# The third of seven gated products done by halves in the later chunks of a hashed-attention and relu-squared kernel

## The chip, the cores and the metric

The kernel runs on one core of a Trainium2 chip. The metric is the device time of one execution in microseconds (us); lower is better. The core has five engines with a queue of instructions each: TensorE (PE, with its weight loads as PEld), VectorE (DVE), ScalarE (ACT), GpSimd (POOL) and SyncE (SP). Each engine takes its own queue strictly in order. SP, ACT and POOL also issue DMA transfers.

## The reference

The input is attention with hash buckets, followed by a gated layer. Queries and keys get a bucket of six sign bits, scores outside the bucket are masked, and the result `x` (3072 tokens by 512) goes through two matrix products with a squared relu between them:

```python
q_bits = (np.einsum('bhsd,dk->bhsk', q, proj) > 0).astype(np.int64)
...
mask = q_bucket[:, :, :, None] == k_bucket[:, :, None, :]
scores = np.where(mask, scale * np.matmul(q, k.transpose(0, 1, 3, 2)), -1000000000.0)
...
attn = exp(scores - max) / sum
x = np.matmul(attn, v)            # (4, 8, 768, 64) -> (3072, 512)
h = x @ w_in                      # 512 x 2048
r = np.maximum(h, 0.0)
out = (r * r) @ w_out             # 2048 x 512
```

All of it is in fp32. The kernel also looks at how large queries and keys are; where they are too large for its fast way, a flag (`slow`) sends it to a general path behind it. With these inputs the flag stays zero.

## The kernel before

The program has an attention stage (to about 318 us) and then three chunks of 1024 tokens. Each chunk has a **gated stage**, `h = x @ w_in` with the squared relu, and an **output stage**, `project`, the product with `w_out`.

**Products by halves.** A matrix product is cut into halves in all three sizes and done with seven products instead of eight (Winograd's form of Strassen's method). The function `product` writes them as `add(...)` number 0, 1, 4, 3, 5, 6, 2 in order of time, between copies on ScalarE (`one`, `two`, `five`, `three`) and sums on VectorE. A chunk's gated stage has 8 units `r`; a unit is a block of 128 hidden columns from each half of the hidden layer. In chunk 0 a unit is one `product` (`hidden`). In chunks 1 and 2 units come in pairs, `r = n` and `r = 4 + n` for n = 0 to 3 (`hidden_pair`, L1047): five of the seven products are done as they are, with factors from `w_unit`, and two of them (number 1 and number 2) are cut by halves once more (`inner_steps`, L996), for both units of the pair at once, with 7 matmuls 256 columns wide instead of 4 that are 512 wide. The inner steps stand between the outer products, so that copies on ScalarE are done by the time their accumulator is used again. Each inner product needs sums of weight blocks, which `factor_units(n)` (L957) makes once, in chunk 0's output stage: two loads on GpSimd's queue (L961), four sums on VectorE (L587 to L590, `sums_a`), four writes on GpSimd's queue to `w_in_49` in DRAM (L970). `load_inner` fetches them on SP's queue, one pair ahead. `sums_inner` (L986) makes the matching sums of `x`, four VectorE operations 256 wide per product.

**Output stage.** It is cut twice by halves too: seven outer products k = 0 to 6, here called output products, each of seven inner products of 16 matmul records (8 matmuls, each counted twice by the profile). Weights come as tiles `leaf`, seven in a ring, loaded on ScalarE's queue. Within an output product, in VectorE's program order, stand: in chunk 0 and for k = 1 to 4 the factor sums of `factor_units(k - 1)`; then the `hook`, which stands behind the first two inner products and holds `minus(y21, y21, t2)` (L1258), needed by the seventh and last inner product of the same k, and `inner_sums(k + 1)`, needed by the next output product; then sums of the accumulators (L1132). After k = 0 and k = 2 come two long differences and the inner sums of k + 2.

**What sets the order.** The whole program stands in `tc.manual_schedule()`: each engine runs its instructions in the order of the source. Tiles with a name come from pools with a fixed number of buffers (`bufs`); a tile of the same name waits until the earlier one in its buffer has been read. So PSUM tiles `acc0`, `acc1`, `acc2` have two buffers each, and `spare` one of two banks. A DMA that overwrites a tile waits until DMAs that read the tile have landed, and it holds up what is behind it on its queue.

**Guard.** `load_peak` fetches queries and keys in 32 pieces on GpSimd's queue and `peak` reduces them to their largest magnitude on VectorE (L877), two pieces per unit in chunks 1 and 2. `guard` multiplies the two largest and sets the flag.

The functions below are those of the kernel before that the change touches.

Of the kernel before, what the change touches and what calls it, by code (L numbers as in the profile page):

```python
# [8 lines left out]
FP32 = mybir.dt.float32  # L9
# [6 lines left out]
ALU = mybir.AluOpType  # L16
# [18 lines left out]
def kernel(  # L35
# [49 lines left out]
    w_in_49 = p_d.tile([NQ, P, 2, 7, P], FP32, name="w_in_49")  # L85
# [571 lines left out]
    with tc.manual_schedule():  # L657
# [168 lines left out]

        def product(n, w, at, bt, c11, c12, c21, c22, hook=None):
# [13 lines left out]
            def keep(of, name):  # L841
                t = p_r.tile([P, 512], FP32, name=name)[:, 0:w]
                nc.scalar.copy(out=t, in_=acc[of])  # L843
                return t
# [45 lines left out]
        def guard():  # L890
# [3 lines left out]
            for w in range(2):  # L894
# [8 lines left out]
                out=slow, in0=most[:, 0:1], scalar1=most[:, 1:2], scalar2=PLAIN / (scale * D),  # L903
# [52 lines left out]

        def factor_units(n):  # L957
# [9 lines left out]
            for lo, hi, t in (  # L967
                (0, 2, src[0]), (2, 3, src[1][:, :, 1:2]), (3, 5, sums[0]), (5, 7, sums[1])
            ):
                nc.gpsimd.dma_start(out=w_in_49[n, :, :, lo:hi], in_=t)  # L970

        def load_inner(i, n):

            if n < NQ:
                w_inner[i, n] = []
                for j, name in enumerate((("sum0", "sum3"), ("sum2", "sum1"))[n % 2]):
                    t = p_y.tile([P, 4, QN], FP32, name=name).rearrange("p a (b c) -> p (a b) c", c=P)
                    nc.sync.dma_start(out=t[:, 0:7], in_=w_in_49[n, :, j])
                    w_inner[i, n].append(t)

        def quarters_x(i, j):

            b = xs[i][0][:, 2:4, 0:HN] if j == 0 else xs[i][0][:, 0:2, HN:NCH]
            return b[:, 0, 0:QN], b[:, 0, QN:HN], b[:, 1, 0:QN], b[:, 1, QN:HN]

        def sums_inner(i):  # L986

            t_inner[i] = [p_y.tile([P, NQ, QN], FP32, name=f"t{m}", bufs=2) for m in range(2)]
# [7 lines left out]
        def inner_steps(i, n, j):  # L996
# [5 lines left out]
            if i not in snaps:  # L1002
                o = [p_y.tile([P, HN], FP32, name="o", bufs=NOUT) for _ in range(2)]
                snaps[i] = [o[m // 2][:, m % 2 * QN:(m % 2 + 1) * QN] for m in range(4)]
            one, two, three, five = snaps[i]

            def mul(out, a, b, start, stop):
                nc.tensor.matmul(  # L1008
                    out=out, lhsT=w[:, a], rhs=b, start=start, stop=stop, skip_group_check=True
                )  # L1010
# [10 lines left out]
            def step_1():  # L1021
                hs["a2"] = spare("acc3")[:, 0, 0:QN]
# [24 lines left out]
        def hidden_pair(i, n, half):  # L1047

            r = half * NQ + n
            w, bt = w_unit.pop(i * NR + 2 * n + half), factors_x(i)  # L1050
            acc = {m: ps_m.tile([P, 512], FP32, name=f"acc{m}") for m in (0, 2)}

            def add(to, a, b, first, last):
                for f in range(NFT // 2):
                    nc.tensor.matmul(  # L1055
                        out=acc[to], lhsT=w[:, PLACE[a], f], rhs=bt[b](f),
# [4 lines left out]
            def keep(of, name):  # L1061
                t = p_r.tile([P, 512], FP32, name=name)
                nc.scalar.copy(out=t, in_=acc[of])
                return t

            if half == 0:
                load_inner(i, n + 1)
                now[0], now[1] = (inner_steps(i, n, j) for j in range(2))
# [539 lines left out]
```

## Time and profile before

| | |
|---|---|
| three runs | 866.06, 866.54, 868.85 us; median 866.54 |
| profiled execution | 866.6 us; span of its instructions 864.4 us; mean granted TensorE clock 0.997 |
| chunk 0: gated stage, output stage | about 317.8 to 414.0, 414.0 to 499.5 us of the span |
| chunk 1: gated stage, output stage | 499.5 to 592.4, 592.4 to 677 us |
| chunk 2: gated stage, output stage | 677 to 770, 770 to 864 us |
| output products of chunk 0 start at | k=2 439.1, k=3 451.2, k=6 487.5 us |

Times in the profile count from the start of the span. A line of a timeline gives the start, the duration, the engine, the line of the source, the operation with its tiles (output, then inputs), the shape, how many such instructions are merged, and in brackets how long the engine sat idle before and what ended it. A line of the table by windows gives, after the window, the busy time of each engine with its count, then the granted clock, the share of DMA time and the GB/s. "To landing" is the time from a DMA's issue until its data has arrived. L836 and L1055 are the `add` of `product` and of `hidden_pair`, L1008 the inner products, L593 all differences made by `minus`, L1132 all `add_to`.

### The profile page before, as it was taken

The page shows a single profiled execution, that of the slowest core. Times are in us where ns is not written, and L with a number is a line of the kernel's source. Part 1 is how long each engine was busy: PE and PEld are TensorE (multiplying, and loading weights), DVE is VectorE, ACT ScalarE, POOL GpSimd, SP SyncE. Part 2 cuts the span into 40 slices and gives each one's busy share as a digit, 9 for nine tenths or more (in the row PEclk, how much of TensorE's full clock was granted, in tenths as well). Part 3 has the DMA queues.
Part 4 walks back from the last instruction along what each step waited for, and adds up shares of the span by engine and source line. Part 5 has one row for each costly group of instructions (what it writes and reads, how often), then busy time and mean ns, then how long its engine had stood idle before and what let it go on. Part 6 is the DMA issues. An engine that isn't in the chain of part 4 may idle for free.

```text
span 864.4 us, 16743 instructions
## 1 busy us (share of the span) xinstructions
PE 851.6 (99%) x6548; PEld 519.3 (60%) x6548; DVE 749.3 (87%) x1005; ACT 362.3 (42%) x648; POOL 169.4 (20%) x284
## 2 busy tenths in 40 slices
PE   8999999999999999999999999999999999999996
PEld 3544444444444444444788855557888655568885
DVE  5899999999999998988879978888799688888875
ACT  5787777888777752222111133332111233321110
POOL 1321111123221102642132211112001111100003
PEclk9999999999999999999999999999999999999998
DMA  9677898879997518999788854537757645355565
GB/s 206 128 144 153 175 188 197 209 159 252 251 218 210 192 48 281 317 320 291 279 280 261 178 167 157 176 118 261 249 157 191 161 156 175 119 161 159 147 185 99
DMA packets 226629, 168.03 MB, mean 194 GB/s; under 512 B 167112, under 2 KB 184848, under 8 KB 226544
## 3 DMA queue, kind: packets, MB, share of 16 engines
q1 hardware_dynamic: 187744, 87.19, 40.5%
q0 software_dynamic: 16416, 41.95, 15.8%
q10 hardware_dynamic: 22384, 37.76, 14.3%
q8 instruction: 53, 0.87, 0.4%
q14 instruction: 32, 0.26, 0.1%
HBM read 124.52 MB, written 41.68 MB: 192 GB/s over the span
## 4 chain that ended last, share of the span: by engine, by line
PE 95%; DMA 2%; DVE 1%; issue 0%; POOL 0%; ACT 0%; POOLq 0%; DVEq 0%; ACTq 0%
PE acc L836 39%; PE st L430 17%; PE acc L1055 16%; PE xo L485 14%; PE acc L1008 6%; PE tot L534 2%; PE hash L360 1%; DMA leaf<-w_out 1%; DMA bits<-signed 1%; DVE bits L410 0%; DVE feat L344 0%; DVE total L473 0%; POOL bits L396 0%; DVE total L468 0%; PE xo L360 0%
## 5 line engine op out<-in xcount | busy, mean ns | idle before, releaser
L436 ACT ACTIVATE e<-st 128x768 f32<-128x768 f32 x192 | 155.6, 811 | 59.6 <-PE st L430 56.7
L430 PE MATMUL st<-feat 64*64 64x384 f32 x1536 | 157.5, 483 | 1.0 <-DVE feat L329 1.0
L485 PE MATMUL xo<-e,v_nat 64*64 64x385 f32 (+1 forms) x1520 | 157.2, 483 | 0.0
L836 PE MATMUL acc<-b,leaf 128*128 128x256 f32 x600 | 133.4, 379 | 0.4 <-DMA leaf<-w_out 0.4
L836 PEld LDWEIGHTS acc<-b,leaf 128*128 128x128 f32 x600 | 113.7, 190 | 17.2 <-issue 1.4
L473 DVE TENSOR_TENSOR total<-total,e 128x1536 f32<-128x1536 f32 x64 | 111.8, 1747 | 4.4 <-ACT e L436 2.8
L396 POOL DMA_DIRECT2D bits<-signed x120 | 62.2, 522 | 217.1 <-ACT signed L385 217.1
L485 PEld LDWEIGHTS xo<-e,v_nat 64*64 64x64 f32 (+1 forms) x1520 | 56.5, 133 | 67.2 <-issue 59.0
L1055 PE MATMUL acc<-t_x,w_unit 128*128 128x512 f32 x192 | 90.2, 592 | 0.0
L430 PEld LDWEIGHTS st<-feat 64*64 64x64 f32 x1536 | 56.0, 133 | 39.1 <-issue 33.7
L836 PE MATMUL acc<-t,leaf 128*128 128x256 f32 x336 | 76.2, 380 | 0.0
L836 PEld LDWEIGHTS acc<-t,leaf 128*128 128x128 f32 x336 | 63.7, 190 | 9.1 <-DVE t L593 0.5
L920 DVE SCALAR_TENSOR_TENSOR b<-h 128x512 f32<-128x512 f32 x96 | 65.7, 691 | 3.1
L430 PE MATMUL st<-bits 64*64 64x384 bf16 x768 | 65.2, 325 | 0.9 <-DMA bits<-signed 0.5
L1055 PE MATMUL acc<-x,w_unit 128*128 128x512 f32 x128 | 60.1, 592 | 0.0
L836 PE MATMUL acc<-x,w_unit 128*128 128x512 f32 x128 | 56.5, 593 | 0.0
L1055 PEld LDWEIGHTS acc<-t_x,w_unit 128*128 128x128 f32 x192 | 36.5, 190 | 28.9 <-issue 26.8
L836 PE MATMUL acc<-b_t,leaf 128*128 128x256 f32 x240 | 53.8, 379 | 0.0
L1153 POOL DMA_DIRECT2D out_dram<-h x26 | 16.9, 656 | 174.1 <-DVE h L1146 167.0
L843 ACT COPY two<-acc 128x256 f32<-128x256 f32 (+1 forms) x29 | 12.5, 432 | 87.8 <-PE acc L836 78.4
L836 PEld LDWEIGHTS acc<-b_t,leaf 128*128 128x128 f32 x240 | 45.5, 190 | 6.2
L873 POOL DMA_DIRECT2D raw_qk<-in_q_dram x32 | 17.4, 543 | 162.4 <-DVE peaks L877 162.4
(155 smaller groups left out, 1194.8 us busy)
## 6 DMA issues: line engine op xcount, KB each, us to landing
leaf<-w_out ACTq DMA_DIRECT2D x142, 256.0 KB, 3.1
w_unit<-w_in SPq DMA_DIRECT2D x16, 640.0 KB, 3.9
raw<-in_moe_w_in_dram SPq DMA_DIRECT2D x8, 1024.0 KB, 6.9
raw<-in_moe_w_out_dram SPq DMA_DIRECT2D x8, 1024.0 KB, 7.2
w_unit<-w_in SPq DMA_DIRECT2D x8, 896.0 KB, 9.3
w_out<-sums POOLq DMA_DIRECT2D x16, 448.0 KB, 7.9
sum<-w_in SPq DMA_DIRECT2D x16, 448.0 KB, 5.0
v_nat<-in_v_dram SPq DMA_DIRECT2D x16, 384.0 KB, 5.1
```

The lines of the kernel that those rows point to most:

```text
L396: nc.gpsimd.dma_start(out=t[h * D:h * D + NBITS + 1, w, c * HS:(c + 1) * HS], in_=signed[at:at + NBITS + 1, h],)
L430: nc.tensor.matmul(out=st[k * HK:(k + 1) * HK, h, 0:HS], lhsT=src[1][rows, key], rhs=src[0][rows, cut], start=first, stop=not first, skip_ ...
L436: nc.scalar.activation(out=key_of(pr, kt)[:, :, i, 0:HS], in_=st[:, :, 0:HS], func=ACTF.Exp, scale=scale)
L473: nc.vector.tensor_tensor(out=totals[pr], in0=totals[pr], in1=e, op=ALU.add)
L485: return nc.tensor.matmul(out=outs[pr][h * D:(h + 1) * D, c, 0:HS + 1], lhsT=nat[pr, "v_nat"][rows, h, kt * D:(kt + 1) * D], rhs=key_of(pr ...
L534: done = nc.tensor.matmul(out=spares[pr][g * 32:(g + 1) * 32, c2, 0:QS], lhsT=ones[rows], rhs=totals[pr][rows, h, c, c2 * QS:(c2 + 1) * QS ...
L836: nc.tensor.matmul(out=acc[to], lhsT=a(i), rhs=b(i), start=first and i == 0, stop=last and i == n - 1, skip_group_check=True,)
L873: nc.gpsimd.dma_start(out=raw_qk[i][:, w], in_=flat[:, i * n:(i + 1) * n])
L920: nc.vector.scalar_tensor_tensor(out=out, in0=h, scalar=0.0, in1=h, op0=ALU.max, op1=ALU.mult)
L1008: nc.tensor.matmul(out=out, lhsT=w[:, a], rhs=b, start=start, stop=stop, skip_group_check=True)
L1055: nc.tensor.matmul(out=acc[to], lhsT=w[:, PLACE[a], f], rhs=bt[b](f), start=first and f == 0, stop=last and f == NFT // 2 - 1, skip_group_ ...
L1153: queue.dma_start(out=out[at, m0 + a * 32:m0 + (a + 1) * 32].rearrange("(c i) j -> i c j", i=32), in_=ot[a * 32:(a + 1) * 32].rearrange("i ...
```

## The change

In chunks 1 and 2 product number 6 of a pair is done by halves too, as a third set of inner steps. `now` holds three sets, A (product 1), B (product 6) and C (product 2), and `hidden_pair` is rewritten: per half four outer products (0, 3, 4, 5), with the steps of A and the first of B in the first half, the rest of B and those of C in the second. Product 3 gets an accumulator of its own (`acc2`), and `two = two + five` on VectorE replaces the summing of 3 and 6 in PSUM. The inner steps use `acc1` and `acc2` in place of two `acc1`, and the two banks of `spare` in turn. The differences `b_t`, `b12` and the first inner sums of the output stage, which followed each unit, move into `hidden_pair`, in the second half ahead of the last gates.

The factors of product 6 have a tile `t2` of their own with one buffer, and a rhythm of their own in chunk 0's output stage: in the hook of k come, in this order, the four sums of third k - 2 (`sum_third`), its three writes on GpSimd's queue (`keep_third`), and the two loads of third k - 1 (`load_third`). Pairs fetch them into two `leaf` buffers, on SP's queue, and for a chunk's first pair on ScalarE's queue in the hook of k = 6. `sums_inner` makes twelve sums instead of eight. `w_unit` is loaded with four blocks instead of five. The copies `two` and `five` have one buffer instead of two.

The guard's reduction moves from VectorE to ScalarE: `peak` squares a piece in place, with a sum along the row, four times per half; the flag's threshold is changed to fit sums of squares.

```diff
-    w_in_49 = p_d.tile([NQ, P, 2, 7, P], FP32, name="w_in_49")
+    w_in_49 = p_d.tile([NQ, P, 3, 7, P], FP32, name="w_in_49")
...
-            m = 7 if n < NR else 5
+            m = 7 if n < NR else 4
...
+        KEPT = dict(one=2, two=1, three=2, five=1)
...
-        def peak(i):
-
-            nc.vector.tensor_reduce(
-                out=peaks[:, :, i], in_=raw_qk.pop(i), axis=AXL.X, op=ALU.max,
-                apply_absolute_value=True,
-            )
+        def peak(i, w):
+
+            t = raw_qk[i][:, w]
+            nc.scalar.activation(
+                out=t, in_=t, func=ACTF.Square, accum_out=peaks[:, w, i:i + 1]
+            )
...
+        def load_third(n):
+
+            t = p_y.tile([P, NQ, QN], FP32, name="t2").rearrange("p a (b c) -> p (a b) c", c=P)
+            thirds[n] = t
+            for j in range(2):
+                nc.gpsimd.dma_start(
+                    out=t[:, 2 * j:2 * j + 2], in_=w_in_7[j * NQ + n, :, PLACE[6]]
+                )
+
+        def sum_third(n):
+
+            t = thirds[n]
+            sums_a(*(t[:, m] for m in range(8)))
+
+        def keep_third(n):
+
+            t = thirds.pop(n)
+            for lo, hi, a in (0, 2, 0), (2, 3, 3), (3, 7, 4):
+                nc.gpsimd.dma_start(out=w_in_49[n, :, 2, lo:hi], in_=t[:, a:a + hi - lo])
...
+        def load_third_inner(i, n, queue):
+
+            if n < NQ:
+                ts = [p_y.tile([P, NQ, P], FP32, name="leaf", bufs=NLEAF) for _ in range(2)]
+                for m, t in enumerate(ts):
+                    hi = min(4 * m + 4, 7)
+                    queue.dma_start(out=t[:, 0:hi - 4 * m], in_=w_in_49[n, :, 2, 4 * m:hi])
+                w_inner[i, n].append(lambda a: ts[a // 4][:, a % 4])
...
-                a0, a1 = (ps_m.tile([P, 512], FP32, name="acc1")[:, 0:QN] for _ in range(2))
+                a0, a1 = (ps_m.tile([P, 512], FP32, name=f"acc{m}")[:, 0:QN] for m in (1, 2))
...
-                hs["a2"] = spare("acc3")[:, 0, 0:QN]
+                hs["a2"] = last
...
+            A, B, C = (now[c] for c in "ABC")
+            add(acc, 0, "11", True, False)
+            one = keep(acc, "one")
+            if half == 0:
+                A[0]()
+            else:
+                B[2]()
+                C[0]()
+                A[4](1, b11[:, r], one)
+                B[4](0, b12[:, r0], now["two"])
+            mark()
+            other = ps_m.tile([P, 512], FP32, name="acc2")
+            add(other, 3, "t1", True, True)
+            five = keep(other, "five")
+            if half == 0:
+                A[1]()
+            else:
+                B[3]()
+                C[1]()
+                minus(b_t[:, r0], b12[:, r0], b11[:, r0])
+                minus(b12[:, r0], b22[:, r0], b12[:, r0])
+            mark()
+            add(acc, 4, "t2", False, False)
+            two = keep(acc, "two")
+            if half == 0:
+                A[2]()
+                B[0]()
+                A[4](0, b11[:, r], one)
+                nc.vector.tensor_tensor(out=two, in0=two, in1=five, op=ALU.add)
+            else:
+                C[2]()
+                nc.vector.tensor_tensor(out=two, in0=two, in1=five, op=ALU.add)
+                B[4](1, b12[:, r], two)
+                minus(b_t[:, r], b12[:, r], b11[:, r])
+                inner_sums(0, slice(n, n + 1))
+                C[4](0, b21[:, r0], now["three"])
+            mark()
+            add(acc, 5, "t3", False, True)
+            three = keep(acc, "three")
+            if half == 0:
+                A[3]()
+                B[1]()
+                gate_sum(b22[:, r], three, five)
+            else:
+                C[3]()
+                gate_sum(b22[:, r], three, five)
+                minus(b12[:, r], b22[:, r], b12[:, r])
+                C[4](1, b21[:, r], three)
+            mark()
...
                     if k + 1 < 7 and k not in (1, 3):
                         inner_sums(k + 1)
+                    if i == 0 and 1 < k <= NQ + 1:
+                        sum_third(k - 2)
+                        keep_third(k - 2)
+                    if i == 0 and 0 < k <= NQ:
+                        load_third(k - 1)
                     if k == 6 and more:
+                        load_third_inner(i + 1, 0, nc.scalar)
                         sums_inner(i + 1)
```

More of the change, by code (lines that the diff above doesn't have):

```diff
@@ L1061, in keep, with mark @@
             def keep(of, name):
-                t = p_r.tile([P, 512], FP32, name=name)
-                nc.scalar.copy(out=t, in_=acc[of])
-                return t
+                t = p_r.tile([P, 512], FP32, name=name, bufs=KEPT[name])
+                nc.scalar.copy(out=t, in_=of)
+                return t
+            marks = iter([(2 * ((i - 1) * NR + 2 * n + half) + m, c) for m in range(2) for c in range(2)])
+            def mark():
+                peak(*next(marks))
             if half == 0:
@@ L1081, in hidden_pair @@
-            steps[2 - half]()
-            if half == 0:
-                put(0, b11[:, r], one)
-            add(2, 6, "22", False, True)
-            gate_sum(b12[:, r], acc[2], two)
-            steps[3 - half]()
-            if half:
-                put(0, b21[:, n], now["three"])
-            add(0, 5, "t3", False, True)
-            three = keep(0, "three")
-            gate_sum(b22[:, r], three, five)
-            if half:
-                steps[3]()
-                put(1, b21[:, r], three)
@@ L1098 @@
+            mark()
[11 more added lines that the diff above has]
+            mark()
+            now["two"], now["three"] = two, three
         OUTER = (0, b11), (5, b12), (3, b_t), (6, b22), (1, b21), (4, b11), (2, b_t)
@@ L1342 @@
                     hidden_pair(i, s // 2, s % 2)
[L1343 removed]
+                if i == 0:
+                    minus(b_t[:, r], b12[:, r], b11[:, r])
                 if i == 0 and r in WHEN:
```

56 lines of the change are left out of this document (25 added, 31 removed).

## The prediction

> **What bounds the kernel now.** I read the busy times first, then the busy times of chosen windows, then the timelines of TensorE, VectorE and GpSimd in the first output stage, then the time to landing of GpSimd's DMAs there. The page:
>
> ```profile
> PE 851.6 (99%) x6548; PEld 519.3 (60%) x6548; DVE 749.3 (87%) x1005; ACT 362.3 (42%) x648; POOL 169.4 (20%) x284
> ```
>
> TensorE has no gap to win back, so only less matmul work can help. Two windows show how much cover VectorE gives (after PE and PEld the columns are DVE, ACT and POOL):
>
> ```profile
> 460.00:470.00 10.00, 10.00 (x48) 8.79 (x48) 9.69 (x20) 1.12 (x3) 4.37 (x7) 1.00 0.88 295
> ...
> 522.90:546.10 23.20, 23.20 (x70) 12.91 (x69) 19.65 (x34) 7.82 (x19) 4.26 (x8) 1.00 0.49 165
> ```
>
> The second is one pair of the gated layer in a later chunk: VectorE has 3.5 us to spare. The first lies in chunk 0's output stage: 0.3 us to spare in 10. The change also works there. GpSimd's timeline, around output product k=2 (439.1 to 451.2):
>
> ```profile
> 444.90 1.41 POOL L970 DMA_DIRECT2D w_in<-h  x2 [0.43 <-DVE h L589]
> 446.03 1.40 POOL L961 DMA_DIRECT2D h<-w_in  x2
> ...
> 452.97 0.70 POOL L970 DMA_DIRECT2D w_in<-h  x1 [0.39 <-DMA h<-w_in]
> 459.96 1.41 POOL L970 DMA_DIRECT2D w_in<-h  x2 [6.29 <-DVE h L589]
> 461.10 1.39 POOL L961 DMA_DIRECT2D h<-w_in  x2
> ```
>
> GpSimd asks for the next factors (L961) as soon as the previous ones are written, here 12.5 us before VectorE sums them. It works strictly in order and blocks on each wait. VectorE at the same time:
>
> ```profile
> 443.51 0.43 DVE L587 TENSOR_TENSOR h<-h 128x256 f32<-128x256 f32 x1 [3.78 <-DMA h<-w_in]
> ...
> 450.65 4.49 DVE L593 TENSOR_TENSOR b_t<-b,b 128x2048 f32<-128x2048 f32 x2
> 455.05 1.22 DVE L593 TENSOR_TENSOR t<-b 128x1024 f32<-128x1024 f32 x1
> ...
> 458.58 0.42 DVE L587 TENSOR_TENSOR h<-h 128x256 f32<-128x256 f32 x1
> ...
> 460.05 1.22 DVE L593 TENSOR_TENSOR b<-b,t 128x1024 f32<-128x1024 f32 x1
> ```
>
> The factor sums (458.58, four) stand ahead of `minus(y21, y21, t2)` (460.05), which feeds the last inner product of k=3. TensorE:
>
> ```profile
> 451.19 3.62 PE L836 MATMUL acc<-b,leaf 128*128 128x256 f32 x16
> 454.64 3.62 PE L836 MATMUL acc<-t,leaf 128*128 128x256 f32 x16
> 458.10 8.80 PE L836 MATMUL acc<-b,leaf 128*128 128x256 f32 x40
> ```
>
> 16 records take 3.45 us; the first 16 of the 40 are two other inner products, so the last one of k=3 starts at 461.55, and y21 is ready at 461.27: 0.28 us of slack. The same reading gives slack of 3.3, 2.8, 3.7 and 2.3 us at k=2, 4, 5, 6. Landing of L970's writes, then of L961's loads:
>
> ```profile
> DMA to landing us min/median/max: 2.7/3.6/5.8
> ```
> ```profile
> DMA to landing us min/median/max: 5.6/6.2/13.0
> ```
>
> **TensorE's work.** The third product of a pair cost 8 records 512 wide; four take 1.72 us (timeline, L1055), so 3.44. Its seven inner products are 14 records 256 wide, 0.215 each: 3.01. Times 8 pairs (two chunks of four): **-3.44 us**. This stands only if TensorE stays the bound.
>
> **The new rhythm in a pair.** Laid out from 0, with 1.72 us an outer and 0.43 an inner product, a pair takes 22.8 us. VectorE loses four peak reductions (0.947 each) and gains two adds of 0.69 and three of 0.42: 19.65 - 3.79 + 2.64 = 18.5 us, so it has more room. Its longest run of work starts at 20.85 and lasts 9.3 us with the starts 0.34 to 0.72 apart that the timeline shows; the next pair's first sum is then done at 7.75 of its time, and TensorE wants that accumulator at 8.17: no wait, 0.4 to spare. ScalarE gains 8 squares and 5 copies of 0.375 a pair. A square 128x384 with a sum is in no row: between the copy 256 wide (0.37) and the reduction 768 wide (0.95); I take 0.5, nearest to the exponential's 0.81 at 768. The narrowest gap between due copies is 1.3 us, so nothing waits. One new tight place: in the second half `two` is copied with only one inner step (0.86) before the accumulator goes on. From the timeline, end to copy 0.21, copy 0.59: 0.06 to spare, without the hand-back. A wait of 0 to 0.13 us, 8 times: 0 to 1.0, I take **+0.3**. The output sums moved ahead of the last gates take away a stall of 0.14 us at the start of the two later output stages (773.41, where 16 records take 3.59 instead of 3.45): **-0.3**. The unit loads shrink from 640 to 512 KB and 448 KB a pair come on top, at a DMA share of 0.49: hidden. These loads go on SP's queue behind the other inner loads, into leaf buffers whose leaves are read by then; for a chunk's first pair they go on ScalarE's queue, where they wait for the first two leaves of k=6 (read by 490.9) ahead of a copy due at 492.83: hidden. GpSimd's peak loads now wait for ScalarE's squares, which come 6 us or more ahead of the next use (3.3 to land): hidden. With one buffer, `two` and `five` are copied again 4.4 us after their last reading at the closest (490.12, 494.56): hidden, and 0.5 us late, under 0.7 of cover, after the delays below.
>
> **Chunk 0's output stage.** Three things are added. On GpSimd, per n, two loads into `t2` and three writes from it, where `t2` has one buffer. On VectorE four sums 128x128 a time, in the hooks of k=2 to 5: between a reduction of one column (0.28) and the sums of 256 (0.42, starts 0.34 to 0.45 apart); starts of 0.2 to 0.3, 0.95 for four. In the hook of k=6 four more sums of 256, 1.6 us. What matters is the order on GpSimd: writes of third n, which wait for VectorE's sums; loads of third n+1, which wait until those writes have landed, the buffer being the same; and only then the next two loads of L961, which the next factor sums wait for. The early request is gone. Step by step:
>
> - k=1, 2: two more issues (0.57 each) and 256 KB go ahead of L961's loads: the sums at 443.51 come 1.7 us later (1.1 by the issues alone, 2.1 with 256 KB at 267 GB/s). y21 is ready at 447.9, due at 449.5: no wait. The inner sums for k=3 end at 451.3, the first third-sums at T = 452.25.
> - k=3: write at T+0.1, landed 3.6 later, then four issues 0.57 apart, the last landed 6.2 after issue: T+11.66 = 463.9. VectorE alone would be there after 1.0 (three sums) + 4.4 + 3.53 = 461.2. Factor sums 1.47, y21 1.2: 466.6 against 461.55. TensorE waits **5.1**.
> - k=4: third-sums end at 467.45, factors land at 479.1 (VectorE would be free at 467.45 + 4.55 + 2.4 = 474.4), y21 at 481.8 against 461.55 + 12.09 + 5.1 = 478.7: **3.1**.
> - k=5: no factors any more; VectorE alone: 3.5 + 0.95 + 4.2 + 2.4 + 1.2, y21 at 493.9, due then: 0.
> - k=6: 3.5 + 0.95 + 8.8 + 1.2: y21 at 508.3, due at 506.0: **2.3**.
> - Start of chunk 1: the second accumulator of k=6 is read after 12 small sums (4.8) and 1.2 us, at 514.1. The new pair takes that buffer for its second outer product, at 510.0 + 2.6: **1.6**. The old pair took the other buffer first.
>
> Together **+12.1 us**. The last two steps follow from VectorE having no slack after 450 (3.78 us of idle were its only reserve). Bounds: with the shortest landings (2.7, 5.6) each of the two rounds is 1.5 us shorter, +9.1; with 5.8 and 6.2 + 1.5 each is 3.7 longer, +19.5, and the median rows are nearest. After chunk 1's output stage, with idle of 3.0, 1.9, 1.0 and 0.8 us and no factors to sum, the 1.6 us meet room: 0.
>
> The Trainium skill (DMA: Bandwidth & Descriptors, section Anatomy of one DMA) gives such a transfer as about 2.0 us plus its bytes at 436 GB/s; an estimate from that page for 256 KB is 2.6 us, where the rows have 3.6 and 6.2. Were it so, the rival of short transfers below would hold; the rows decide against it.
>
> **Sum** on the profiled execution: 866.6 (span 864.4 and 2.2 around; median 866.54, the same) - 3.44 + 0.3 - 0.3 + 12.1 = **875.3 us**.
>
> **Rivals.**
> - VectorE alone: landings short enough that no factor sum waits, but its own additions still shift it, since it is full. Waits then 2.35 at k=3, 0.7 at k=6, 1.6 at the start of chunk 1: 4.65, and 867.9 us. It needs T+9 instead of T+11.66 at k=3 and T+7 at k=4. Against it: no load of L961 landed in under 5.6.
> - Short transfers, not slower: if every transfer of GpSimd lands in 2.7 us, the shortest row of the writes, the factors come in at 440.5, in the idle time before 443.51, and all third-sums but the last two find room; 0.6 is left at k=6 and 1.6 after: 866.6 - 3.4 + 2.2 = 865.4. The point from which it decides is a landing under about 3.5 us. Were even the last two waits covered, the saving alone would stand: 863.2. For it: writes landed in 2.7; against it the loads' 5.6.
> - ScalarE too slow: if a square takes over 1.3 us, `two` is late in each pair; at 2.0 us by 0.7 x 8 = 5.6 on top: 881. For it: no row has this form; against it: 0.81 for twice the columns.
>
> **How the numbers follow.** GpSimd's queue as worked out 0.74; VectorE alone 0.08; short transfers 0.08 (0.03 of it at 863.2); ScalarE 0.07; no effect anywhere 0.03. The time is that of the first. Of its bounds, 872.4 to 882.8, the upper end is unlikely. The range 867.7 to 880.5 takes in VectorE alone and leaves out under 0.2. A difference under 0.3% (2.6 us) is about what a measurement can't tell from no change: faster than 864.0 gets 0.06, within 0.10 (the rest of short transfers, part of VectorE alone), slower 0.84.
>
> **What would show it.** In the changed profile VectorE should wait about 2.7 us and 4.7 us for DMA of L961's tile ahead of the third and fourth factor sums; GpSimd's load of `t2` should wait for a DMA some 3.6 us; TensorE should wait for VectorE's y21 (L593) by about 5, 3, 0 and 2 us at k=3 to 6 and 1.6 us early in chunk 1. Both gated stages of later chunks should take 91.2 us instead of 92.8 each, with no waits but tenths at `two`. The forecast is wrong if the loads of L961 are issued before the third's writes have landed, if y21 comes before 463, or if a pair takes over 23 us.

## The result and the profile after

The changed kernel takes 872.01 us (median of 7 runs, 871.37 to 876.39); the kernel before took 866.65 beside it: a ratio of 1.0068, 95% interval 1.0049 to 1.0087. It is slower by 5.4 us, where 8.7 were forecast. The profiled execution took 875.85 us (span 873.8); five of the seven runs lie near 872, so two more profiles are read beside it below. They are called the second and the third profile here, this one the first.

Span, busy times and the chain that ended last, from the page of the changed kernel:

```profile
span 873.8 us, 17006 instructions
...
PE 852.8 (98%) x6596; PEld 531.8 (61%) x6596; DVE 749.9 (86%) x1037; ACT 408.2 (47%) x816; POOL 180.3 (21%) x304
...
PE 82%; DMA 6%; DVE 5%; issue 3%; POOL 1%; ACT 0%; SPq 0%; ACTq 0%; DVEq 0%; POOLq 0%
```

TensorE has less to multiply, yet its busy time went from 851.6 up to 852.8: some matmuls became slower. And 6% of the chain that ended last are now DMAs. One pair of chunk 1, as the window of the kernel before was shown:

```profile
535.24:558.12 22.88, 22.88 (x76) 13.98 (x75) 18.95 (x35) 13.59 (x40) 4.26 (x8) 1.00 0.52 176
```

22.88 us without a gap, against 23.20. The pairs do what the change says, and the loss must lie elsewhere. TensorE's timeline around k=3 of chunk 0's output stage (start, duration; in brackets the idle time before and what ended it):

```profile
458.35 3.62 PE L838 MATMUL acc<-b,leaf 128*128 128x256 f32 x16
468.12 7.56 PE L838 MATMUL acc<-b,leaf 128*128 128x256 f32 x24 [6.15 <-issue]
475.52 3.62 PE L838 MATMUL acc<-t,leaf 128*128 128x256 f32 x16
478.97 8.80 PE L838 MATMUL acc<-b,leaf 128*128 128x256 f32 x40
```

TensorE stands still for 6.15 us ahead of the last inner product of k=3. The 24 records that follow take 7.56 us where 24 records after a short wait take 5.42. At k=4 (the row of 40) nothing waits. VectorE's timeline tells what the trace only calls "issue":

```profile
465.33 0.42 DVE L587 TENSOR_TENSOR h<-h 128x256 f32<-128x256 f32 x1 [3.98 <-DMA h<-w_in]
...
466.80 1.22 DVE L593 TENSOR_TENSOR b<-b,t 128x1024 f32<-128x1024 f32 x1
```

The second row is y21 of k=3; it ends at 468.02, and TensorE goes on at 468.12, 0.10 us later (0.10 in the second and third profile too). Ahead of it VectorE waited 3.98 us for a factor load. GpSimd, which issues that load:

```profile
452.71 0.54 POOL L994 DMA_DIRECT2D w_in<-t  x1 [3.50 <-DVE t L590]
457.16 1.07 POOL L981 DMA_DIRECT2D t<-w_in  x2 [3.91 <-DMA w_in<-t]
458.22 1.07 POOL L965 DMA_DIRECT2D h<-w_in  x2
464.40 0.72 POOL L974 DMA_DIRECT2D w_in<-h  x1 [5.11 <-DMA h<-w_in]
...
472.09 1.07 POOL L981 DMA_DIRECT2D t<-w_in  x2 [2.27 <-DMA w_in<-t]
473.15 1.06 POOL L965 DMA_DIRECT2D h<-w_in  x2
476.36 0.72 POOL L974 DMA_DIRECT2D w_in<-h  x1 [2.15 <-DMA h<-w_in]
```

This is the chain of the forecast: a third's last write waits 3.50 us for VectorE's sums (L590), the load of the next third waits 3.91 for that write to land, and only then come the factor loads (L965), at 458.22. In the kernel before they were issued at 446.03. In the next round (from 472.09) the same chain runs faster. The landing of L965's loads, first those of 458.22, then those of 473.15:

```profile
DMA to landing us min/median/max: 5.9/6.2/6.5
```
```profile
DMA to landing us min/median/max: 2.9/3.2/3.5
```

At the start of chunk 1, on TensorE:

```profile
508.38 1.88 PE L1096 MATMUL acc<-x,w_unit 128*128 128x512 f32 x4
512.28 1.13 PE L1049 MATMUL acc<-x,sum 128*128 128x256 f32 x4 [2.02 <-DMA sum<-w_in]
513.24 3.44 PE L1096 MATMUL acc<-t_x,w_unit 128*128 128x512 f32 x4
516.48 1.21 PE L1049 MATMUL acc<-t,sum 128*128 128x256 f32 x4
```

The wait of 2.02 us is for the first factor tile of chunk 1, a transfer on SyncE's queue that the forecast does not name. The four records at 513.24 then take 3.44 us instead of 1.88.

To compare profiles that begin chunk 0's output stage 3 us apart, I use a stretch: from that stage's first matmul (414.01 in the kernel before) to the third row of inner products in chunk 1's first pair (506.42). It is 92.41 us before and 104.28 here: +11.87. The pieces shown come to as much: 6.15 + 2.02 of waits, 2.14 (7.56 - 5.42) and 1.56 (3.44 - 1.88) of slow matmuls. That they meet it exactly is chance: the kernel before has a wait of its own in this stretch, 0.4 us for a weight tile (`leaf`), that this profile has not, and smaller slow rows are left out here.

### The profile page after: what moved, and what is told of

Read it like the earlier page. It is cut to its first block, busy times and chain, and to the rows that moved or that the text cites. A ratio compares the mean times of both kernels' runs of the same rounds, so it can differ in the third digit from the quotient of the medians.

```text
span 873.8 us, 17006 instructions
## 1 busy us (share of the span) xinstructions
PE 852.8 (98%) x6596; PEld 531.8 (61%) x6596; DVE 749.9 (86%) x1037; ACT 408.2 (47%) x816; POOL 180.3 (21%) x304
## 4 chain that ended last, share of the span: by engine, by line
PE 82%; DMA 6%; DVE 5%; issue 3%; POOL 1%; ACT 0%; SPq 0%; ACTq 0%; DVEq 0%; POOLq 0%
PE acc L838 27%; PE st L430 17%; PE xo L485 14%; PE acc L1096 13%; PE acc L1049 8%; DMA h<-w_in 3%; PE tot L534 2%; PE hash L360 1%; DMA w_in<-t 1%; DMA sum<-w_in 1%; DMA qk_nat<-in_k_dram 1%; DVE b L593 1%; DMA bits<-signed 1%; DVE t L593 1%; DVE h L1216 0%
## 5 line engine op out<-in xcount | busy, mean ns | idle before, releaser
L838 PE MATMUL acc<-b,leaf 128*128 128x256 f32 x600 | 135.5, 384 | 6.2 <-issue 6.2
L1096 PE MATMUL acc<-t_x,w_unit 128*128 128x512 f32 x192 | 92.4, 604 | 0.0
L838 PE MATMUL acc<-x,w_unit 128*128 128x512 f32 x128 | 56.5, 593 | 0.0
L1096 PEld LDWEIGHTS acc<-t_x,w_unit 128*128 128x128 f32 x192 | 36.1, 191 | 27.3 <-issue 23.5
L845 ACT COPY one<-acc 128x256 f32<-128x256 f32 (+1 forms) x29 | 12.5, 431 | 85.8 <-PE acc L838 61.8
```

The lines of the kernel that those rows point to most:

```text
L838: nc.tensor.matmul(out=acc[to], lhsT=a(i), rhs=b(i), start=first and i == 0, stop=last and i == n - 1, skip_group_check=True,)
L1096: nc.tensor.matmul(out=to, lhsT=w[:, PLACE[a], f], rhs=bt[b](f), start=first and f == 0, stop=last and f == NFT // 2 - 1, skip_group_check ...
```

## Further profiles of the kernels as they are

> The changed kernel once more, unchanged, for a second profile. Its seven timed runs fall into two groups, 871.4 to 872.3 us and 875.9 to 876.4 us, and the profile shown is of the upper group. GpSimd's queue as the cause: the wait of TensorE at k=3 is there again (6.15 us in the first profile), between 4 and 6.2 us; a profile of the lower group differs by how long TensorE ran at a lower clock after its waits, or by the wait at the start of chunk 1. Rival, a wait elsewhere that the first profile happens not to show: another place appears.

Measured: 874.42 us, a single run. The stretch is 103.27 (+10.86).

> The changed kernel as it is, three rounds on the chip of the other runs (the earlier run meant for this was the kernel before). Median 872 to 874; in the profile a wait of 4 to 6 us for k = 3's inner block behind a VectorE wait of 3 to 4 us for the fourth... factor tile, slow matmuls behind it, and a start of chunk 1 that is 8 to 10 us later than in the kernel before, counted from the start of the output stage.

Measured: 872.23 us (870.75 to 874.03, 4 runs) against 867.88, a ratio of 1.0066 (1.0042 to 1.0091); the profiled run took 870.78, its stretch 101.26 (+8.85). TensorE's waits in the two, from the timelines, with the groups that follow:

```profile
467.84 6.92 PE L838 MATMUL acc<-b,leaf 128*128 128x256 f32 x24 [4.88 <-issue]
507.85 3.20 PE L838 MATMUL acc<-b_t,leaf 128*128 128x256 f32 x8 [2.01 <-issue]
510.84 2.38 PE L1096 MATMUL acc<-x,w_unit 128*128 128x512 f32 x4
```
```profile
464.51 7.10 PE L838 MATMUL acc<-b,leaf 128*128 128x256 f32 x24 [4.29 <-issue]
504.24 1.97 PE L838 MATMUL acc<-b_t,leaf 128*128 128x256 f32 x8 [1.54 <-issue]
508.10 1.13 PE L1049 MATMUL acc<-x,sum 128*128 128x256 f32 x4 [0.18 <-DMA sum<-w_in]
510.08 1.98 PE L1096 MATMUL acc<-t_x,w_unit 128*128 128x512 f32 x4 [0.85 <-DVE tmp L1202]
```

So the wait at k=3 is there in each profile (6.15, 4.88, 4.29), with none at k=4; the forecast's waits at k=6 and for VectorE's reading of the last accumulator (L1202) show when k=3 costs less. In the third profile the factor loads of k=3 landed in 4.2 us (median) and VectorE waited 2.05 for them. Over the three profiles the landing at k=3 (6.2, 5.2 and 4.2 us) goes with the time (875.85, 874.42, 870.78); three points are a hint and no proof.

> The changed kernel as it is, on the chip of the other runs, for a median beside theirs. By the two looks so far (a wait at k = 3 of 6.15 and 4.88 us, 2.2 and 1.6 us of slow matmuls behind it) the spread comes from how long the transfers on GpSimd's queue take: the median is 872 to 874, and the wait at k = 3 is 4 to 6 us again with slow matmuls behind it, none at k = 4. A look with a time near 871.5 should have a wait near 4 at k = 3 or none at k = 6.

The file that ran under this label was the kernel before. It took 868.01 us (866.47 to 871.86, 10 runs), with a stretch of 92.48: the stretch of the kernel before repeats within 0.1 us, while its output stage begins 2.3 us later. What its text above expects of the changed kernel is to be read against the run before it.

## The experiments

**The pairs alone.** In chunk 0's output stage no thirds are summed, loaded or written; the pairs read the second product's factors in their place:

```diff
-                    queue.dma_start(out=t[:, 0:hi - 4 * m], in_=w_in_49[n, :, 2, 4 * m:hi])
+                    queue.dma_start(out=t[:, 0:hi - 4 * m], in_=w_in_49[n, :, 1, 4 * m:hi])
...
-                    if i == 0 and 1 < k <= NQ + 1:
-                        sum_third(k - 2)
-                        keep_third(k - 2)
-                    if i == 0 and 0 < k <= NQ:
-                        load_third(k - 1)
```

> Left out: the making of the third factors in chunk 0's output stage (the four sums, the writes and the loads of each third); the pairs read another product's factors in their place, so the output is not the reference's. All cost in chunk 0's output stage and its aftermath: no wait at k=3, none over 0.5 us at the start of chunk 1 (the last accumulator sum is then read at 501.4, due at 502.1), and only the pairs' saving is left: 866.6 - 3.44 + 0.64 (0.08 a pair at the copy of two, as the first profile shows) - 0.3 = 863.5 us. Rival, the pairs' new rhythm is no gain by itself: 866 us or more.

Measured: 863.83 us (863.21 to 865.33, 10 runs) against 867.11, a ratio of 0.9962 (0.9943 to 0.9982). Its stretch is 92.96 (+0.55), and at k=3 one small wait is left:

```profile
461.47 5.42 PE L838 MATMUL acc<-b,leaf 128*128 128x256 f32 x24 [0.22 <-issue]
```

The new rhythm of the pairs is a gain of 3.3 us, and the making of the thirds costs all the rest, some 8.4 us at the medians (872.23 - 863.83), or 7.6 where each is first compared with the kernel before that ran beside it (867.88 and 867.11).

**The factor loads first.** The same work, but the next product's factor loads are issued ahead of the thirds' writes and loads on GpSimd's queue (`load_factors` holds the two loads that stood in `factor_units`):

```diff
+                if i == 0 and k == 1:
+                    load_factors(0)
...
+                    if i == 0 and 0 < k < NQ:
+                        load_factors(k)
                     if i == 0 and 1 < k <= NQ + 1:
                         sum_third(k - 2)
                         keep_third(k - 2)
```

> The two loads for the next factor sums are issued ahead of the third's writes and loads, as early as in the kernel before; nothing else changes. GpSimd's queue as the cause: VectorE no longer waits for these loads ahead of the third and fourth factor sums, the wait at k=3 falls from 6.15 us to about 0.5 (0.95 us of third sums less 0.28 of slack), with 0.7 at k=6 and 2 at the start of chunk 1: 866.7 us. Rival, VectorE's added sums are the cause: the order on GpSimd makes no difference, 872 us.

Measured: 868.08 us (864.74 to 872.45, 10 runs), ratio 1.0002 (0.9976 to 1.0028); the profiled run took 865.18. TensorE's longest waits in it, at k=3, at k=6 and for chunk 1's first factor tile:

```profile
461.58 5.42 PE L838 MATMUL acc<-b,leaf 128*128 128x256 f32 x24 [0.50 <-issue]
498.88 1.97 PE L838 MATMUL acc<-b_t,leaf 128*128 128x256 f32 x8 [0.80 <-issue]
503.15 1.13 PE L1055 MATMUL acc<-x,sum 128*128 128x256 f32 x4 [0.58 <-DMA sum<-w_in]
```

With all transfers and sums kept and only their order changed, the wait at k=3 falls from between 4.3 and 6.2 us to 0.50, and some 4 us come back at the median (872.23 - 868.08; 3.4 by the kernel before beside each). VectorE, which kept the sums, has no wait for a factor load at k=3 or k=4 in this profile. So the order of GpSimd's queue is the cause of the wait at k=3, and of about half of the cost at the median. It does not explain all: 4.2 us above the run without thirds remain (2.0 between the two profiled runs), with a spread of 7.7 us.

**TensorE kept busy.** Four idle products of 512 columns into a spare bank ahead of the last inner product of k=3, to see what the slow matmuls behind the wait cost:

```diff
+                def fill():
+                    void = spare("fill")[:, 0]
+                    for _ in range(4):
+                        nc.tensor.matmul(out=void, lhsT=ident, rhs=b[:, 0], start=True, stop=True)
...
+                    fill if (i, k) == (0, 3) else None,
```

> Four idle matmuls 512 wide (3.44 us, result unused) are put on TensorE ahead of the last inner product of k=3, inside its wait. If the slow matmuls after the wait (24 records in 7.56 us instead of 5.34) come from the idle time, the idle time left is under 3 us, the matmuls run at full rate and 2.2 us go: about 870 us. If the idle time has nothing to do with it, or if the wait is no wait for VectorE: 872 us or, where the fill does not fit, up to 875.

Measured: 873.94 us (871.31 to 876.03, 10 runs), ratio 1.0074 (1.0051 to 1.0097); stretch +9.69. TensorE's timeline:

```profile
461.31 3.60 PE L1352 MATMUL fill<-b,ident 128*128 128x512 f32 x8
465.86 5.42 PE L838 MATMUL acc<-b,leaf 128*128 128x256 f32 x24 [0.95 <-issue]
479.93 5.42 PE L838 MATMUL acc<-b,leaf 128*128 128x256 f32 x24 [1.75 <-issue]
506.42 3.01 PE L838 MATMUL acc<-b_t,leaf 128*128 128x256 f32 x8 [2.03 <-issue]
```

The records behind k=3 run at full rate, as the text above expected where the idle time is the cause, but the 870 us that went with it are a miss: TensorE now waits 1.75 us at k=4 and 2.03 at k=6, and no time is won. In this profile the y21 of k=4 ends at 479.84 and TensorE goes on at 479.93. So VectorE's chain sets the end there, and matmuls that are slow at k=3 lie beside its lateness.

**No sums of the thirds.** VectorE's four sums of each third are left out, and the third's last write takes loaded blocks in their place:

```diff
         def sum_third(n):
-            t = thirds[n]
-            sums_a(*(t[:, m] for m in range(8)))
+            pass
...
-            for lo, hi, a in (0, 2, 0), (2, 3, 3), (3, 7, 4):
+            for lo, hi, a in (0, 2, 0), (2, 3, 3), (3, 7, 0):
```

> Leaves out VectorE's four sums of each third; the last write of a third takes loaded blocks in place of sums, so all transfers and their order on GpSimd's queue stay, and the output is another. Theory (GpSimd's queue waits 3.50 us for VectorE's sums of a third, and the factor loads of the next product stand behind): the write is issued some 3.4 us earlier at k = 3, the factor loads too, so the wait of 6.15 (4.88 in the second look) comes down to 1.8 to 2.7 us with fewer slow matmuls behind it, the one at k = 4 stays 0, chunk 1's start stays at 1 to 2: the fifth inner group some 5 to 7 us after the kernel before's instead of 12, the median 867 to 869. Rival (the landing of the write and the loads alone makes the wait, 3.9 and 5.1 us, and VectorE's sums are hidden): the wait at k = 3 stays at 5 to 6 and the time at 872.

Measured: 872.98 us (869.20 to 874.65, 6 runs), ratio 1.0058 (1.0038 to 1.0078); the profiled run took 870.65, stretch +7.25. Its waits at k=3 and k=4 on TensorE, then VectorE's wait for the factors of k=4:

```profile
464.42 7.11 PE L838 MATMUL acc<-b,leaf 128*128 128x256 f32 x24 [2.71 <-issue]
479.17 5.42 PE L838 MATMUL acc<-b,leaf 128*128 128x256 f32 x24 [0.74 <-issue]
```
```profile
476.38 0.42 DVE L587 TENSOR_TENSOR h<-h 128x256 f32<-128x256 f32 x1 [5.12 <-DMA h<-w_in]
```

In the profile the wait at k=3 is 2.71, at the end of what the queue theory gave (1.8 to 2.7). But the median did not fall to 867 to 869: a miss. The third's last write no longer waits for VectorE, but the load behind it now waits 5.77 us for the writes to land (3.91 in the first profile), so more than half of the lead is lost; and at k=4 VectorE waits 5.12 us for the factors. In this order the landings behind each other hold VectorE up with or without its sums of the thirds, and at the median leaving these out wins nothing.

**Thirds in other rounds.** On top of the factor loads first: loads of the thirds at k=0, 1, 3, 4, sums at k=1, 3, 4, 5, and the first factor loads at k=0.

```diff
+        LOADED, SUMMED = (0, 1, 3, 4), (1, 3, 4, 5)
...
-                if i == 0 and k == 1:
-                    load_factors(0)
...
-                    if i == 0 and 0 < k < NQ:
+                    if i == 0 and k < NQ:
                         load_factors(k)
-                    if i == 0 and 1 < k <= NQ + 1:
-                        sum_third(k - 2)
-                        keep_third(k - 2)
-                    if i == 0 and 0 < k <= NQ:
-                        load_third(k - 1)
+                    if i == 0 and k in SUMMED:
+                        sum_third(SUMMED.index(k))
+                        keep_third(SUMMED.index(k))
+                    if i == 0 and k in LOADED:
+                        load_third(LOADED.index(k))
```

> On top of the run with the factor loads issued first: the third factors' work gets a rhythm of its own in chunk 0's output stage, so that no product carries both a late factor sum and third sums. Loads of third 0 to 3 in the rounds of k = 0, 1, 3, 4, sums and writes in k = 1, 3, 4, 5 (before: loads in k = 1 to 4, sums in 2 to 5); VectorE stood idle for 3.8 us in the round of k = 1. Theory (the order of GpSimd's queue and what VectorE holds in front of it): the wait of 0.50 us that was left at k = 3 goes to 0, that of 0.80 at k = 6 stays at 0 to 0.8, chunk 1 starts as there (1.0 us of waits), so that the fifth inner group ends no later than 509 and the median falls from 868.1 to about 866, with less spread. Rival (the landing times of so many transfers beside the leaf loads set the end whatever the order): the spread from 864.7 to 872.5 and the median of 868 stay.

Measured: 867.12 us (864.92 to 870.05, 12 runs), ratio 1.0000 (0.9986 to 1.0014). In the profiled run (865.74) no wait of TensorE is left at k=2 to 6; the one at chunk 1's first factor tile has grown to 1.70 us. The median is 1 us above the theory's 866, and by the ratio it is level with the run that only loads the factors first (1.0002); the spread narrowed from 7.7 to 5.1 us.

**The same with the next chunk's sums in two steps.** `sums_inner(i + 1, (0, 1))` in the hook of k=6, `sums_inner(i + 1, (2,))` after that product.

> The kernel with the thirds in idle rounds, and the sums of x for the next chunk's inner groups in two steps: those of the first two groups stay in the hook of k = 6, the third group's come after that product. VectorE then reads the last accumulators of k = 6 some 1.6 us earlier. Theory: the wait for the accumulator in chunk 1's first pair (0.45 us where the factor loads went first) goes, the one for the factors of the first inner group (0.58) stays or grows by what the other gave up: 0.3 to 0.5 us less than the kernel without the split, about 865.5. Rival: SyncE's transfer of those factors alone sets the start of chunk 1, and the split is worth nothing.

Measured: 866.34 us (864.41 to 870.61, 12 runs), ratio 0.9990 (0.9975 to 1.0004). The 0.8 us to the kernel without the split is not told apart from nothing at these spreads. The profiled run happened to be the longest of the twelve, and shows where it loses its time:

```profile
502.98 3.65 PE L838 MATMUL acc<-b_t,leaf 128*128 128x256 f32 x8 [2.54 <-issue]
```

VectorE waited 0.39, 0.89 and 0.81 us for loads in the rounds of k=4 (the first two) and k=5, 2.09 together, and TensorE waits 2.54 at k=6. In the profile without the split VectorE has no wait after 443.43 in this stage, and TensorE none at k=2 to 6. From there on VectorE is full, and what it waits comes back on TensorE.

**The sums of the thirds on GpSimd.** On top of the factor loads first (`sums_a` now takes an engine):

```diff
-            sums_a(*(t[:, m] for m in range(8)))
+            sums_a(*(t[:, m] for m in range(8)), engine=nc.gpsimd)
```

> The run with the factor loads first, and the four sums of each third on GpSimd in place of VectorE. Theory: from 445 us on VectorE has no slack in chunk 0's output stage (14.6 to 14.9 us busy of each 15 in the kernel before), so whatever is put on it there, or makes it wait, comes back as a wait of TensorE at a product's last inner block. Without the thirds' 0.93 us each the waits of 0.50 at k = 3 and 0.80 at k = 6 go; the first inner group of chunk 1 may still wait 0.6 to 1.7 for its factors. Median 864.5 to 865.5, against 868.1 and 867.1 for the two kernels with the sums on VectorE. GpSimd's own price is not shown by any row yet; up to 3 us per third it stays beside the work. Rival (GpSimd's sums are slow or hold VectorE up, so that the loads behind them on its queue come later): the waits at k = 3 to 5 come back, 868 or more.

Measured: 870.32 us (867.35 to 872.70, 12 runs) against 867.88, ratio 1.0030 (1.0014 to 1.0047): a miss. VectorE has no wait after 444.12 there, but TensorE does:

```profile
463.49 5.42 PE L838 MATMUL acc<-b,leaf 128*128 128x256 f32 x24 [1.44 <-issue]
506.66 1.39 PE L1055 MATMUL acc<-x,sum 128*128 128x256 f32 x4 [3.23 <-DMA sum<-w_in]
507.84 3.36 PE L1102 MATMUL acc<-t_x,w_unit 128*128 128x512 f32 x4
```

The wait for chunk 1's first factor tile is 3.23 us, with slow matmuls behind it. SyncE's queue, last rows of the output stage:

```profile
480.04 20.79 SPq L1229 DMA_DIRECT2D out_dram<-h  x16
501.07 2.11 SPq L1008 DMA_DIRECT2D sum<-w_in  x2
```

The two factor loads leave at 501.07, behind 16 output writes. VectorE's last transpose for those writes ended at 497.82.

**That load one product earlier.** The same, with the load of the first tile ahead of k=5's output writes (its buffer, `sum0`, is free after k=4):

```diff
-                if k == 6 and more:
-                    load_inner(i + 1, 0)
+                if k > 4 and more:
+                    load_inner(i + 1, 0, (k - 5,))
```

> The same, and the first factor tile of the next chunk's first pair is loaded ahead of the sixth product's output writes on SyncE's queue (its buffer is free after the fifth product), one product earlier than before. Theory: the waits for that tile seen at the start of chunk 1 (2.02 in the changed kernel, 0.87, 0.58 and 1.70 in three variants) come from its place behind output writes that wait for VectorE; it goes, and at most the wait for the last accumulators (0.2 to 0.5) stays: 0.5 to 1.5 us less than without, 863.5 to 864.5, the level of the run that makes no thirds. Rival (a tight place elsewhere, the accumulators of k = 6 read by VectorE, ends at the same time): no difference to the run without.

Measured: 865.83 us (864.65 to 867.11, 12 runs) against 867.88, ratio 0.9982 (0.9971 to 0.9992): 4.5 us below the kernel without this edit, and with a spread of 2.5 us. Two waits of TensorE are left in the profile between k=3 and chunk 1's first pair, both short:

```profile
462.69 5.42 PE L838 MATMUL acc<-b,leaf 128*128 128x256 f32 x24 [0.42 <-issue]
503.85 1.98 PE L1103 MATMUL acc<-t_x,w_unit 128*128 128x512 f32 x4 [0.36 <-DVE tmp L1209]
```

SyncE issues the tile at 487.15 now. This version computes all of the output and beats both kernels: by 2.1 us the one before, by about 6.4 the changed one (872.23 in the same session). It ends 1.3 us above the upper end of what was expected, and 2.0 above the run without thirds. How much of it is due to the sums on GpSimd is not shown: the early load was not tried with the sums on VectorE.

**The early load alone in the changed kernel.** The same edit on the changed kernel, nothing else.

> The changed kernel with one edit: the first factor tile of the next chunk's first pair is loaded one product earlier, ahead of the sixth product's output writes on SyncE's queue. All of GpSimd's order stays. Theory: in the changed kernel the wait for that tile at the start of chunk 1 (2.02 in the first look, 0.18 in the third) ends at nearly the same time as VectorE's reading of the last accumulators (0.85 in the third look), because VectorE is late by its waits in the rounds before; so the edit alone brings 0 to 1 us, median 871.5 to 872.5, with a wait for the accumulators of 0.5 to 2 us in place of the one for the tile, and the wait of 4 to 6 us at k = 3 as it is. Rival (the tile's place in SyncE's queue is a cost of the change by itself, as large as between the two kernels with GpSimd's sums, 870.3 against 865.8): some 868.

Measured: 872.11 us (870.39 to 872.97, 7 runs) against 867.94, ratio 1.0044 (1.0025 to 1.0064), as expected. The wait for the tile is gone; the one for VectorE's last reads is there instead, with 1.15 us at k=6 ahead of it, and the wait at k=3 has stayed:

```profile
466.69 7.11 PE L838 MATMUL acc<-b,leaf 128*128 128x256 f32 x24 [4.49 <-issue]
...
511.87 1.98 PE L1097 MATMUL acc<-t_x,w_unit 128*128 128x512 f32 x4 [1.31 <-DVE tmp L1203]
```

The place in SyncE's queue that cost 4.5 us in the kernel with GpSimd's sums costs nothing measurable in the changed kernel: there VectorE is late, and its last reads end about when the tile comes.

## Why the prediction came out as it did

**Right.** The sign, the place and the chain. The factor loads come behind a write's landing (GpSimd's wait for it 3.91, 4.23 in the third profile; 3.6 forecast), the factor sums wait for them (3.98 and 2.05; 2.7 forecast), y21 is late, and k=3 waits 6.15, 4.88 and 4.29 us (5.1 forecast). Reordering the queue takes the wait away, and the chain with it. Of the three signs of being wrong none came: the factor loads stand behind the landed write, y21 of k=3 ends at 464.4 or later in each profile (463 was the limit), and a pair takes 22.88 us (23). The saving of the pairs was given as -3.44, and as 863.2 us where nothing is lost; the run without thirds gave -3.3 and 863.83.

**Off in size.**
- "k=4: 3.1". No profile has a wait there; VectorE's wait ahead of the fourth factor sums was 1.38, 2.96 and 2.65 us, where 4.7 were forecast. The step took 6.2 us for the factor loads of each round. In the round of k=4 they landed in 3.2, 4.5 and 4.3 us (medians of the three profiles), the write ahead of them in 2.4 to 2.6 instead of 3.6. In the second and third profile a part of the 3.1 is hidden as well: y21 of k=4 is ready only 0.2 and 0.7 us before it is due, and the slow matmuls behind k=3's wait had put that off by 1.5 and 1.7 us. In the first profile it is ready 2.4 us early, with 2.1 of slow matmuls, so nothing is hidden there. Why those transfers landed faster was not tried.
- "k=6: 2.3". 0 in the first profile, 2.01 and 1.54 in the others. In the first TensorE is late by itself: it gets there 0.1 us after y21 (506.59 and 506.47).
- "Start of chunk 1: 1.6", for the accumulator alone. The first profile has 2.02 for a factor tile, the second none, the third 0.18 + 0.85. The accumulator's wait is real (0.85, and 1.31 once the tile is early), but I overlooked SyncE: the load of chunk 1's first factor tile stands behind k=5's output writes, which wait for VectorE's transposes.
- `two`: "+0.3". One group of L1096 in each pair takes 1.96 instead of 1.88, 0.08 times 8: 0.64.
- ScalarE's square, "I take 0.5": 0.533 as a group mean, with a separate read of its sum behind it, 0.19 to 0.21. GpSimd's next loads of queries and keys wait for it, but the chain that ended last has ScalarE at 0%.
- Rounding: by the forecast's own terms its bounds are 872.3 and 882.7 (it has 872.4 and 882.8), and the last accumulator of k=6 is read at 514.3 (it has 514.1). Nothing hangs on this.

**Left out.** Slow matmuls behind a long wait: 3.7 us in the first profile; the forecast put them at nothing. In that profile the sum met the stretch (12.1 forecast, 11.87 measured) by luck: they took the place of the waits at k=4 and k=6. At the median the cost of the thirds is some 8 us (8.4, or 7.6 by the kernel before beside each) and not 12.1, and that is where the forecast of 875.3 is too high. By the third profile, the nearest to the median of the three, the term that was mis-sized is that of k=4: 0 for 3.1; k=3 with its slow matmuls has 5.97 for 5.1, k=6 1.54 for 2.3, the start of chunk 1 1.03 for 1.6.

**The rivals.** VectorE alone (867.9) did not happen: VectorE waited 2 to 4 us for the factors of k=3 in each profile. Short transfers fell too; the loads of k=3 landed in 4.2 to 6.2 us, above the 3.5 at which it decides. The kernel with the factor loads first has VectorE alone as its case; its median, 868.1, is near the 867.9, but its profile has 0.50 us at k=3 where that rival gave 2.35, so the nearness of the numbers shows little.

**Open.** Why SyncE gave out its last loads 3.2 us after the transpose (497.82 to 501.07) with GpSimd's sums, and 0.8 us after it (497.67 to 498.50) with VectorE's. And why the median of the run with the factor loads first (868.08) lies 2.9 us above its profiled run: its longer runs have no profile. With that, the half of the thirds' cost that the order of the queue does not explain stays open in its parts.

## What to carry to other kernels

When new work goes onto a queue that blocks in order, write down for each instruction what it waits for and who stands behind it: a write that waits for a sum, and a load that waits for that write because both use one buffer, cost as much here (some 4 us) as the whole change saves in its pairs (3.3), and the early request behind them was lost. Put requests that feed the critical chain first. When one wait is taken away, search for a second that ends at the same time before judging the edit: here the early load was worth nothing in the changed kernel, and 4.5 us in one where VectorE waits for no load after 444 us.

## What the runs showed of the hardware

**A wait of two microseconds slows the matmuls behind it.** The granted TensorE clock in windows of the changed kernel (the column before the DMA share), after the wait of 6.15, well after it, and after the wait of 2.02:

```profile
468.00:476.00 8.00, 7.88 (x27) 6.62 (x28) 7.59 (x18) 0.37 (x1) 3.95 (x8) 0.72 0.67 210
476.00:484.00 8.00, 8.00 (x39) 7.04 (x38) 6.65 (x11) 1.12 (x3) 4.01 (x6) 1.00 0.91 302
...
513.00:517.00 4.00, 4.00 (x8) 1.84 (x8) 2.65 (x6) 1.27 (x4) 0.00 (x0) 0.57 0.49 77
```

In all profiles above, in this part of the program, waits up to 1.75 us (0.95, 1.15, 1.31, 1.44, 1.54, 1.70, 1.75) were followed by records at full rate, and waits from 2.01 us on (2.01, 2.02, 2.03, 2.54, 2.71, 3.23 and all longer ones) by records that took longer, 1.5 to 2.1 us more in all, whatever the length of the wait. The filled run, where y21 of k=3 was late too (ready at 465.76, due at 461.31) but the fill left a wait of only 0.95, had no slow records there. The Trainium skill (TensorE: Matmul & The Clock Gate, Part 1) says that the clock falls to half after an idle window of about 3.4 us and comes back after some 3.4 us of work. Half rate for 3.4 us is a loss of 1.7 (an estimate from that page), which the traces agree with; the idle time needed was shorter here, 2.0 us.

**Transfers of one size land in 2.9 to 7.4 us.** L965's loads of 256 KB on GpSimd's queue: 5.9 to 6.5 and 2.9 to 3.5 within one execution, up to 7.4 in the second profile. The estimate of 2.6 us for 256 KB that the forecast worked out from the Trainium skill (DMA: Bandwidth & Descriptors, Anatomy of one DMA) was not reached by any of them.

**GpSimd adds 128x128 in 0.44 us and more.** Its sums of the thirds took 0.44 to 0.69 us each for most, 1.3 to 1.5 for a few, against 0.28 on VectorE. The profile's spans on GpSimd are rough.
